# Threshold attention and a quick-GELU feed-forward on one core: the first 512 tokens in one standard block, and a new order of products and scores

## The chip, the core and the metric

The kernel runs on one core of a Trainium2 chip. The metric is device time in microseconds (us) of one execution. The core has five engines with a queue each: TensorE (PE in the profile; its weight loads are PEld), VectorE (DVE), ScalarE (ACT), GpSimd (POOL) and SyncE (SP, which here only starts transfers). Each engine works through its own list of instructions in the order in which the program was built, and waits on semaphores for the others. So an instruction that isn't ready holds up all that stand behind it on its engine.

## The reference

Attention in which only the scores within `tau` of their row's maximum count, and then a feed-forward with the quick GELU. The weights are float64, all else is float32.

```python
def _attn_ref(q, k, v, tau):             # batch 8, heads 8, 576 tokens, head size 64
    scores = q @ k.transpose(0, 1, 3, 2) / np.sqrt(q.shape[-1])
    thresh = np.max(scores, axis=-1, keepdims=True) - tau
    scores = np.where(scores >= thresh, scores, -1000000000.0)
    scores = scores - np.max(scores, axis=-1, keepdims=True)
    attn = np.exp(scores)
    attn = attn / (np.sum(attn, axis=-1, keepdims=True) + 1e-09)
    return attn @ v

x = attn_out.transpose(0, 2, 1, 3).reshape(4608, 512)
h = x @ w_in                             # 512 x 2048
g = h * (1.0 / (1.0 + np.exp(-1.702 * h)))
out = g @ w_out                          # 2048 x 512
```

## The kernel before

The work is cut into 32 head pairs (four to a batch) and 18 feed-forward blocks of 256 tokens. For each pair: scores (line 386 for four key tiles of 128, line 379 for the tail of 64 keys), a copy out of PSUM (`keep`, L405), maxima by column (L419 and some small operations), a subtraction of the threshold (`sub`, L489), a mask and an exponential on ScalarE (L500, L504), the product with the values (L518), and the division, which writes the block's input `xT` (`place_x`, L585). The denominators of the first five pairs come from TensorE (`den`, L518 too), later ones from VectorE.

The float64 weights come in 32 pieces of 128 x 512. Each takes two transfers, four VectorE operations (L325, L339, L343, L351) and one on ScalarE (L333). `w_in` is complete first, then `w_out`.

All engines' work is entered as tasks. A task has an engine, an assumed cost, a rank, the tasks it comes after, and the buffers it takes and gives back. When the program is built, a list scheduler plays the tasks through with the assumed costs. Whenever an engine is free it takes the ready task of the lowest rank, and emits its instructions there and then. The assumed costs therefore decide nothing but the order.

```python
limits = {"psA": 3, "psM": 2, "s_m": 8, ...}        # psA: two PSUM banks each; psM: one bank each
...
FIRST, LAST = -9.0, 1000.0                           # feed-forward products rank last on PE
...
def scores(n, t, c):                                 # one half (288 queries) of a key tile, two heads
    ps = psA.tile([P, 2, 512], FP32, name="ps", tag="ps")
    ...
    for h in range(2):
        nc.tensor.matmul(ps[:, h, 0:SH], lhsT=kT[ts(h, D), ts(t, P)],
                         rhs=qT[ts(h, D), ts(c, SH)], start=True, stop=True)
...
def mm1(blk, j, f):                                  # L600: hidden columns j and j+8 share one bank
    if f == 0:
        hidden[j] = psM.tile([P, BANK], FP32, name="hps", tag="mo")
    for c in range(NDC):                             # 4 products of 256 columns
        nc.tensor.matmul(hidden[j][:, ts(f, BLK)], lhsT=w_in[:, c, ds((f * HF + j) * P, P)],
                         rhs=xTs[blk][:, c, :], start=(c == 0), stop=(c == NDC - 1))

def tanh(j): ...                                     # L609, ACT: th <- hidden bank
def gelu(j): ...                                     # L612, DVE: g <- (th + 1) * hidden; frees the bank

def mm2(i, part):                                    # L622: standard second product, 512 columns
    if part == 0:
        acc[i] = psM.tile([P, d_model], FP32, name="ops", tag="mo")
    for j in range(2 * part, 2 * part + 2):
        nc.tensor.matmul(acc[i], lhsT=g[:, j // HF, j % HF, ts(i, HT)], rhs=w_out[:, j, :], ...)
```

The second product of all blocks but the first is done with seven half-size products in place of eight (Winograd's form of Strassen's scheme). The sums of parts of `w_out` that it needs (`t_sum`, L644, the last of them in place) are made once on GpSimd, the sums of parts of `g` (`s_sums`, `s_last`, L649 to L656) in every block.

```python
def product(x, part):                                # L671: one of seven, in two parts of 4 instructions
    left, right, k, o = PRODUCTS[x]
    if x == k and part == 0:
        banks[k] = psM.tile([P, BANK], FP32, name="ops", tag="mo")
    for j in range(4 * part, 4 * part + 4): ...      # 256 columns each

def feed_forward(blk):
    for j in range(HF):
        for f in range(2):
            ffn.append(task("PE", 1.762, LAST, mm1, blk, j, f, after=..., take=("psM",) if f == 0 else (), ...))
        a = task("ACT", 0.6, FIRST, tanh, j, after=ffn[-1:], take=("io",))
        gelus[j] = task("DVE", 0.69, FIRST, gelu, j, after=[a, ...], give=("psM", "io"))
        ...
    if blk < PLAIN:                                  # PLAIN = 1: block 0 takes mm2 and half, then t_sum
        ...
        return
    order = [(P1, 0), (P2, 0), (P1, 1), (P2, 1)]
    order += [(x, p) for x in (P6, P7, P4, P5, P3) for p in range(2)]
    ...                                              # P1 and P2 each take a psM bank at part 0
```

Of the kernel before, what the change touches and what calls it, by code (L numbers as in the profile page):

```python
# [10 lines left out]
FP32 = mybir.dt.float32  # L11
# [4 lines left out]
ALU = mybir.AluOpType  # L16
# [3 lines left out]
P = 128  # L20
# [10 lines left out]
def kernel(  # L31
# [34 lines left out]
    nc = tc.nc  # L66
    B, H, S, D = q.shape
    d_model, d_ff = moe_w_in.shape
    NPAIR = H // 2
# [5 lines left out]
    BLK = 256  # L75
    BANK = 512
# [52 lines left out]
    for x in ("raw0", "raw1", "qkT0", "qkT1", "mb"):  # L129
# [4 lines left out]

    EARLY = {
        "lower_rows": -1.89,
        "values": 0.42,
        "exps": 0.63,
        "load_qk": -0.91,
        "prep": -1.45,  # L140
        "load_v": 1.46,
        "mask": 0.88,
        "over_groups": -1.9,
        "sub": 0.19,
        "one_group": 0.95,
        "one_row": 0.78,
    }
    LATER = {
        "in_groups": 0.38,
        "mask": -1.46,  # L150
        "scores": 1.23,
        "prep": -1.22,
    }
    CV = {
        "cv_end": -0.76,
        "cv_frac": -1.28,
    }

    def task(engine, cost, rank, f, *a, after=(), take=(), give=(), lag=0.06):
# [72 lines left out]
    def own(n, *pools):  # L232
        return tuple(x + "_apart" for x in pools) if n in APART else pools
# [17 lines left out]
    def load_v(n):  # L251
# [11 lines left out]

    WC = 512
    wide = moe_w_in.dtype != FP32
    NWC = d_ff // WC

    pieces = [
        (w_in, moe_w_in, c, x * NWC // 2 + j)
        for j in range(NWC // 2) for x in range(2) for c in range(NDC)  # L270
    ]
    n_in = len(pieces)
    pieces += [(w_out, moe_w_out, c, j) for c in range(NFC) for j in range(d_model // WC)]
    cv, turn = {}, {"w64": 0}
# [99 lines left out]
    def scores(n, t, c):  # L374
        qT, kT = mats[n, 0], mats[n, 1]
        ps = psA.tile([P, 2, 512], FP32, name="ps", tag="ps")
        if t == NKT:
            for i in range(2):
                nc.tensor.matmul(  # L379
                    ps[:, i, 0:SH], lhsT=kd, rhs=qT[:, ts(i, SH)],  # L380
                    start=True, stop=True,
                )
            del mats[n, 0], mats[n, 1]
        else:
            for h in range(2):
                nc.tensor.matmul(  # L386
                    ps[:, h, 0:SH],
                    lhsT=kT[ts(h, D), ts(t, P)], rhs=qT[ts(h, D), ts(c, SH)],
                    start=True, stop=True,
                )  # L390
        pss[n, t, c] = ps

    def keep(n, t, c):
        if t == NKT:
# [222 lines left out]
    def mm2(i, part):  # L617

        if part == 0:
            acc[i] = psM.tile([P, d_model], FP32, name="ops", tag="mo")  # L620
        for j in range(2 * part, 2 * part + 2):
            nc.tensor.matmul(  # L622
                acc[i], lhsT=g[:, j // HF, j % HF, ts(i, HT)], rhs=w_out[:, j, :],
                start=(j == 0), stop=(j == NFC - 1),
            )

    def half(i):
        osbs[i] = work.tile([P, d_model], FP32, name="osb", tag=f"osb{i}", bufs=1)
        nc.scalar.activation(out=osbs[i], in_=acc.pop(i), func=AF.Copy, scale=0.5)


    qa = [[g[:, f, :, ts(h, HT)] for f in range(2)] for h in range(2)]
    qb = [[w_out[:, ts(f, HF), ts(m, HM)] for m in range(2)] for f in range(2)]
# [29 lines left out]
    ]  # L663
    banks = {}

    def product(x, part):
        left, right, k, o = PRODUCTS[x]
        if x == k and part == 0:
            banks[k] = psM.tile([P, BANK], FP32, name="ops", tag="mo")
        for j in range(4 * part, 4 * part + 4):  # L670
            nc.tensor.matmul(  # L671
                banks[k][:, ts(o, HM)], lhsT=left[:, j, :], rhs=right[:, j, :],
                start=(j == 0), stop=(j == HF - 1),
            )

    def read(x):


        if x == P1:
            for i in range(2):  # L680
                osbs[i] = work.tile([P, d_model], FP32, name="osb", tag=f"osb{i}", bufs=1)
        (c11, c12), (c21, c22) = ([osbs[i][:, ts(m, HM)] for m in range(2)] for i in range(2))
        k, h = PRODUCTS[x][2:]
        ps = banks[k][:, ts(h, HM)]
        if x == P1:
            nc.scalar.activation(out=c21, in_=ps, func=AF.Copy, scale=0.5)
            return
        sums = {
            P6: [(c12, c21)], P2: [(c11, c21)], P7: [(c22, c12)], P4: [(c21, c22)],
            P5: [(c12, c12), (c22, c22)], P3: [(c12, c12)],  # L690
        }
        for o, a in sums[x]:
            nc.vector.scalar_tensor_tensor(  # L693
                out=o, in0=ps, scalar=0.5, in1=a, op0=ALU.mult, op1=ALU.add
            )

    def store(blk, i):
        nc.sync.dma_start(out=out[ds(blk * BLK + i * HT, HT), :], in_=osbs[i])
# [37 lines left out]
    BY_PE = 5  # L736
    BY_DMA = 8
    LEAD = 6

    W_IN, W_OUT = (3.04, 0.51), (2.15, 3.32)  # L740
    ready_w, w_loads = [], []
    for i in range(len(pieces)):
        if i < n_in:
# [20 lines left out]

    placed, ffn = {}, []
    last_mm2, t_ready = {}, []
    PLAIN = 1

    def feed_forward(blk):
        b = -(-(blk + 1) * BLK // S) - 1  # L770
# [2 lines left out]
        for j in range(HF):  # L773
            for f in range(2):
                after = ffn[-1:] + xs[-NPAIR:]
                if blk == 0:
                    x = 2 * (j * P // WC) + f
                    after += ready_w[x * NDC : (x + 1) * NDC]
                last = j == HF - 1 and f == 1
                ffn.append(task(  # L780
                    "PE", 1.762, LAST, mm1, blk, j, f, after=after,
                    take=("psM",) if f == 0 else (), give=("xT",) if last else (),
                ))
            a = task("ACT", 0.6, FIRST, tanh, j, after=ffn[-1:], take=("io",))
            gelus[j] = task(
                "DVE", 0.69, FIRST, gelu, j, after=[a, last_mm2.get(j // 4)],
                give=("psM", "io"),
            )
            if blk >= PLAIN and j % 2:
                sums.append(task("POOL", 2.5, FIRST, s_sums, j // 2, after=[gelus[j - 1], gelus[j]]))  # L790
        if blk < PLAIN:
            for i in range(2):
                for p in range(NFC // 2):
                    after = ffn[-1:] + [gelus[2 * p % HF], gelus[2 * p % HF + 1]]
                    if blk == 0:
                        after += ready_w[n_in + 2 * p : n_in + 2 * p + 2]
                    ffn.append(task(
                        "PE", 1.762, LAST, mm2, i, p, after=after,
                        take=("psM",) if p == 0 else (),
                    ))  # L800
                    last_mm2[p // 2 % 2] = ffn[-1]
                a = task("ACT", 0.6, FIRST, half, i, after=ffn[-1:], take=("osb",), give=("psM",))
                task("SP", 0.6, FIRST, store, blk, i, after=[a], give=("osb",), lag=2.2)
            if blk == PLAIN - 1:

                for x in range(4):
                    for k in range(2):
                        after = t_ready[-1:] + (ffn[-1:] if x == 3 else ffn[16 : 17])
                        t_ready.append(task("POOL", 3.2, FIRST, t_sum, x, k, after=after + ready_w[n_in:]))
            return  # L810
        reads = [None] * 7

        order = [(P1, 0), (P2, 0), (P1, 1), (P2, 1)]
        order += [(x, p) for x in (P6, P7, P4, P5, P3) for p in range(2)]
        for x, p in order:
            after = ffn[-1:] + t_ready
            if x in (P1, P2, P4):
                after += [gelus[j] for j in range(4 * p, 4 * p + 4)]
            elif x == P3:
                after.append(lasts[p])  # L820
            else:
                after += sums[2 * p : 2 * p + 2]

            after += [reads[y] for y in range(x) if PRODUCTS[y][2:] == PRODUCTS[x][2:]]
            ffn.append(task(
                "PE", 1.762, LAST, product, x, p, after=after,
                take=("psM",) if x in (P1, P2) and p == 0 else (),
            ))
            last_mm2[p] = ffn[-1]
            if p == 0:  # L830
                continue
            if x == P6:
                lasts = [task("POOL", 1.6, FIRST, s_last, k, after=ffn[-1:]) for k in range(2)]
# [16 lines left out]
    for n in range(NP):  # L850
# [19 lines left out]
        for t in range(NKT + 1):  # L870
            tail = t == NKT
            copies = []
            for c in range(1 if tail else 2):

                a = task(
                    "PE", (0.97 if tail else 0.53) * slow, r, scores, n, t, c,
                    after=[pq, pk] + ([pd] if tail else []) + after,
                    take=("psA", "s_t") if tail else ("psA",) + (own(n, "s_m") if c == 0 else ()),
                    give=own(n, "qkT0", "qkT1") + ("kd",) if tail else (),
                )  # L880
                after = [a]
                copies.append(task("ACT", 0.65, r, keep, n, t, c, after=[a], give=("psA",)))
            mx.append(task("DVE", 0.76 if tail else 1.37, r, in_groups, n, t, ALU.max, after=copies))
        a = task("DVE", 0.78, r, over_tiles, n, ALU.max, after=mx)
        a = task("DVE", 0.78, r, over_groups, n, ALU.max, after=[a])
# [55 lines left out]
            "DVE", 1.1, r, place_x, n, after=[a, pv], take=("xT",) * len(new), give=("psA", "rc")  # L941
        )
        while hp == NPAIR - 1 and (next_blk + 1) * BLK <= (b + 1) * S:
            feed_forward(next_blk)
            next_blk += 1
    run_in_order()

# [29 lines left out]
```

## Time and profile before

| | |
|---|---|
| time of three runs | 1413.49, 1418.3, 1419.67 us (median 1418.3) |
| profiled execution | 1415.12 us, 1413.3 us from first to last instruction |
| mean granted TensorE clock | 0.982 |
| busy share PE, PEld, DVE, ACT, POOL | 95%, 73%, 75%, 44%, 21% |

How to read it: a group of the profile is a source line on an engine with its tiles, the number of records and their mean time. A float32 matrix product instruction leaves two records, so four instructions show as "x8". "Idle before" names what ended a wait. "PEclk" or "granted clock" is the share of full TensorE speed that the chip allowed in a stretch. Times on the timeline count from the first instruction.

### The profile page before, as it was taken

What the parts mean: (1) busy time and instruction counts of PE and PEld (TensorE: products, weight loads), DVE (VectorE), ACT (ScalarE), POOL (GpSimd) and SP (SyncE); (2) the same over time, 40 slices, a digit from 0 to 9 for tenths busy, and PEclk for the clock granted to TensorE, in tenths of its full rate; (3) what the DMA queues carried; (4) which work ended last, traced back from release to release, by engine and by line L of the source; (5) the groups of instructions that cost most, each with busy time, mean ns of one, the idle gap of its engine ahead of it and who ended that gap; (6) DMA issues with size and microseconds to landing.
All of it is one profiled execution on the core that took longest, in us unless ns stands there. A gap on an engine that the chain in (4) does not pass through costs nothing.

```text
span 1413.3 us, 18181 instructions
## 1 busy us (share of the span) xinstructions
PE 1346.5 (95%) x6904; PEld 1028.8 (73%) x6904; DVE 1063.4 (75%) x1780; ACT 628.9 (44%) x805; POOL 303.8 (21%) x388
## 2 busy tenths in 40 slices
PE   5878897999999999999999999999999999999998
PEld 3436546777777777777777777777777777888887
DVE  7998988889998889887888888788876787111111
ACT  6684554555454545454444355454543453100100
POOL 1222263202021222221221202121201212211211
PEclk9989998999999999999999999999999999999999
DMA  8788743131110111111111110111111000000000
GB/s 184 199 288 259 262 120 69 34 62 30 41 26 27 23 34 32 32 27 26 41 26 41 26 41 16 34 26 37 21 41 26 10 15 8 8 16 8 8 15 15
DMA packets 205727, 79.59 MB, mean 56 GB/s; under 512 B 192840, under 2 KB 192840, under 8 KB 205640
## 3 DMA queue, kind: packets, MB, share of 16 engines
q1 hardware_dynamic: 196072, 44.60, 14.8%
q0 software_dynamic: 7200, 33.55, 7.0%
q8 instruction: 54, 0.88, 0.3%
q10 hardware_dynamic: 2368, 0.30, 0.2%
q14 instruction: 33, 0.27, 0.1%
HBM read 68.93 MB, written 9.47 MB: 55 GB/s over the span
## 4 chain that ended last, share of the span: by engine, by line
PE 76%; DVE 18%; DMA 2%; issue 2%; ACT 1%; SPq 0%; POOL 0%; ACTq 0%; DVEq 0%; POOLq 0%
PE hps L600 28%; PE ops L671 27%; PE pv L518 9%; PE ps L386 9%; DVE s_m L489 4%; PE ps L379 2%; DVE part L419 2%; DVE arena L612 2%; DVE s_t L494 1%; DVE mb L463 1%; DVE red L438 1%; DVE w_out L343 1%; DMA arena<-in_moe_w_out_dram 1%; DVE w_in L351 1%; DVE arena L489 1%
## 5 line engine op out<-in xcount | busy, mean ns | idle before, releaser
L600 PE MATMUL hps<-xT,w_in 128*128 128x256 f32 x2304 | 514.9, 382 | 3.1 <-DVE arena L612 2.8
L600 PEld LDWEIGHTS hps<-xT,w_in 128*128 128x128 f32 x2304 | 434.6, 190 | 79.9 <-issue 14.5
L419 DVE TRANSPOSE_TENSOR_REDUCE part<-s_m 128x36 f32<-128x1152 f32 x228 | 304.3, 1357 | 66.1 <-ACT s_m L405 60.8
L671 PE MATMUL ops<-w_out,arena 128*128 128x256 f32 x1088 | 254.3, 386 | 7.6 <-DVE arena L612 7.3
L405 ACT COPY s_m<-ps 128x576 f32<-128x576 f32 x240 | 140.2, 647 | 231.5 <-PE ps L386 229.9
L671 PEld LDWEIGHTS ops<-w_out,arena 128*128 128x128 f32 x1088 | 206.7, 193 | 48.0 <-DVE arena L612 10.1
L609 ACT ACTIVATE th<-hps 128x512 f32<-128x512 f32 x144 | 85.4, 593 | 309.1 <-PE hps L600 300.8
L500 ACT ACTIVATE s_m<-s_m 128x1152 f32<-128x1152 f32 x120 | 136.7, 1156 | 111.0 <-DVE s_m L489 109.7
L612 DVE SCALAR_TENSOR_TENSOR arena<-th,hps 128x512 f32<-128x512 f32 x144 | 97.3, 675 | 117.2 <-ACT th L609 116.1
L671 PE MATMUL ops<-arena 128*128 128x256 f32 x816 | 184.2, 381 | 0.0
L489 DVE TENSOR_TENSOR s_m<-s_m,mb 128x1152 f32<-128x1152 f32 x120 | 176.5, 1509 | 1.9 <-DMA mb<-row 1.6
L649 POOL TENSOR_TENSOR arena<-arena 128x256 f32<-128x256 f32 x68 | 62.2, 914 | 522.5 <-DVE arena L612 519.9
L386 PE MATMUL ps<-qkT 64*128 64x288 f32 x960 | 150.5, 445 | 23.2 <-DVE qkT L362 14.7
L671 PEld LDWEIGHTS ops<-arena 128*128 128x128 f32 x816 | 154.5, 190 | 24.4 <-issue 3.9
L504 ACT ACTIVATE s_m<-s_m,shift,scl 128x1152 f32<-128x1152 f32 x120 | 157.9, 1339 | 1.1
L386 PEld LDWEIGHTS ps<-qkT 64*128 64x128 f32 x960 | 86.8, 196 | 78.3 <-issue 44.2
L693 DVE SCALAR_TENSOR_TENSOR osb<-ops,osb 128x256 f32<-128x256 f32 x119 | 47.8, 413 | 114.5 <-PE ops L671 110.4
L518 PE MATMUL pv<-s_m,v_m 128*64 128x288 f32 x960 | 126.8, 417 | 0.0
L518 PEld LDWEIGHTS pv<-s_m,v_m 128*64 128x64 f32 x960 | 67.7, 140 | 54.7 <-issue 9.6
L367 POOL COPY kd<-qkT 64x64 f32<-64x64 f32 x60 | 13.9, 232 | 314.3 <-DVE qkT L362 312.5
L656 POOL TENSOR_TENSOR arena<-arena 128x512 f32<-128x512 f32 x34 | 49.6, 1461 | 112.9 <-PE ops L671 112.9
L650 POOL TENSOR_TENSOR arena<-arena 128x256 f32<-128x256 f32 x68 | 60.8, 894 | 5.3
(94 smaller groups left out, 971.1 us busy)
## 6 DMA issues: line engine op xcount, KB each, us to landing
out_dram<-osb SPq DMA_DIRECT2D x36, 256.0 KB, 2.0
q_raw<-in_q_dram SPq DMA_DIRECT2D x120, 72.0 KB, 2.3
k_raw<-in_k_dram SPq DMA_DIRECT2D x116, 72.0 KB, 2.3
v_m<-in_v_dram SPq DMA_DIRECT2D x64, 128.0 KB, 2.4
w_out<-in_moe_w_in_dram POOLq DMA_DIRECT2D x12, 512.0 KB, 9.9
arena<-in_moe_w_out_dram POOLq DMA_DIRECT2D x12, 512.0 KB, 6.1
w_out<-in_moe_w_in_dram POOLq DMA_DIRECT2D x12, 511.6 KB, 10.7
arena<-in_moe_w_out_dram POOLq DMA_DIRECT2D x12, 511.6 KB, 7.2
```

Of the source, the lines that this page charges most:

```text
L386: nc.tensor.matmul(ps[:, h, 0:SH], lhsT=kT[ts(h, D), ts(t, P)], rhs=qT[ts(h, D), ts(c, SH)], start=True, stop=True,)
L405: nc.scalar.copy(out=o, in_=pss.pop((n, t, c))[:, :, 0:SH])
L419: nc.vector.tensor_reduce(out=o, in_=i, axis=AXL.X, op=op, apply_transpose=True)
L489: nc.vector.tensor_tensor(out=s, in0=s, in1=mb, op=ALU.subtract)
L500: nc.scalar.activation(out=s, in_=s, func=AF.Prelu, alpha=STEEP)
L504: nc.scalar.activation(out=s, in_=s, func=AF.Exp, scale=scl, bias=shift)
L518: nc.tensor.matmul(o[c][ts(h, D), 0:SH], lhsT=lhsT, rhs=rhs, start=(t == 0), stop=(t == NKT),)
L600: nc.tensor.matmul(hidden[j][:, ts(f, BLK)], lhsT=w_in[:, c, ds((f * HF + j) * P, P)], rhs=xTs[blk][:, c, :], start=(c == 0), stop=(c == N ...
L609: nc.scalar.activation(out=ths[j], in_=hidden[j], func=AF.Tanh, scale=GELU_SCALE / 2)
L612: nc.vector.scalar_tensor_tensor(out=g[:, :, j, :], in0=two(ths.pop(j)), scalar=1.0, in1=two(hidden.pop(j)), op0=ALU.add, op1=ALU.mult,)
L649: nc.gpsimd.tensor_tensor(out=u1, in0=a21, in1=a22, op=ALU.add)
L671: nc.tensor.matmul(banks[k][:, ts(o, HM)], lhsT=left[:, j, :], rhs=right[:, j, :], start=(j == 0), stop=(j == HF - 1),)
```

## The change

It does three things to the order of the work, and sets new ranks and assumed costs for the scheduler.

1. Blocks 0 and 1 become one block of 512 tokens with standard products. Its hidden columns are made in plain order, both blocks' halves into one bank, and `g0` lies over the space of `t4`, `g` and their sums. So one more block than before does without the seven products. The block opens with 128 TensorE instructions of 256 columns that need `w_in` alone (64 before), ahead of any that need `w_out`. The pieces of `w_in` are loaded in that order of columns. Two of the four `t_sum` pairs must now come after the block's last product, since they write where `g0` lay.
2. In the other blocks the first of the seven products is finished (in parts of 4, 3 and 1 instructions) before the second begins, where the two alternated before.
3. From the seventh pair on (`WHOLE = 6`) both halves of a key tile's scores are one task that takes two `psA` buffers, so that TensorE gets its four instructions in one run.

```diff
     EARLY = {
-        "values": 0.42,  "exps": 0.63,  "load_qk": -0.91,  "prep": -1.45,  "sub": 0.19,  "one_row": 0.78,
+        "values": 1.63,  "exps": 1.38,  "load_qk": -1.15,  "prep": -1.35,  "sub": -0.29,
+        "scores": -0.68,  "spread_sums": 0.92,  "sums_by_pe": 1.09,  "in_groups": 0.61,  "keep": -1.15,
...                                       (entries put on one line here; LATER and CV lose entries)
-    pieces = [
-        (w_in, moe_w_in, c, x * NWC // 2 + j)
-        for j in range(NWC // 2) for x in range(2) for c in range(NDC)
-    ]
+    pieces = [(w_in, moe_w_in, c, j) for j in range(d_ff // WC) for c in range(NDC)]
...
+    g0 = arena[:, ds(2 * HF * HM, 2 * NFC * BLK)].rearrange("p (j t) -> p j t", t=2 * BLK)
+    PLAIN = 2
+
+    def mm1_0(j, i):
+        if i == 0:
+            hidden[j] = psM.tile([P, BANK], FP32, name="hps", tag="mo")
+        for c in range(NDC):
+            nc.tensor.matmul(
+                hidden[j][:, ts(i, BLK)], lhsT=w_in[:, c, ts(j, P)], rhs=xTs[i][:, c, :],
+                start=(c == 0), stop=(c == NDC - 1),
+            )
...
-    W_IN, W_OUT = (3.04, 0.51), (2.15, 3.32)
+    W_IN, W_OUT = (3.21, 1.53), (3.16, 2.2)
...
-                    "PE", 1.762, LAST, mm1, blk, j, f, after=after,
+                    "PE", FFU, LAST, mm1, blk, j, f, after=after,          # FFU = 1.722
...
+        for x in range(4):                                  # in first_blocks()
+            for k in range(2):
+                after = t_ready[-1:] + (ffn[-1:] if x > 1 else ffn[2 * NFC : 2 * NFC + 1])
+                t_ready.append(
+                    task("POOL", 3.0, FIRST, t_sum, x, k, after=after + ready_w[n_in:])
+                )
...
-        order = [(P1, 0), (P2, 0), (P1, 1), (P2, 1)]
-        order += [(x, p) for x in (P6, P7, P4, P5, P3) for p in range(2)]
+        order = [(P1, 0), (P1, 2), (P1, 3)]
+        order += [(x, p) for x in range(P2, 7) for p in range(2)]
         for x, p in order:
+            js = ((0, 4), (4, 8), (4, 7), (7, 8))[p]
...
-            for c in range(1 if tail else 2):
+            if tail or n >= WHOLE:
+                cs = range(1 if tail else 2)
                 a = task(
-                    "PE", (0.97 if tail else 0.53) * slow, r, scores, n, t, c,
+                    "PE", (1.2 if tail else 1.35) * slow, r, scores_of, n, t, cs, ...
-                    take=("psA", "s_t") if tail else ("psA",) + (own(n, "s_m") if c == 0 else ()),
+                    take=("psA", "s_t") if tail else ("psA", "psA") + own(n, "s_m"),
...
+            else:
+                for c in range(2): ...                      # as before, assumed cost 0.6
```

## The prediction

> **What bounds the kernel now.** I read the page's busy line first, then a table by stage, then the timeline of TensorE for the stages in which it was idle.
>
> ```profile
> PE 1346.5 (95%) x6904; PEld 1028.8 (73%) x6904; DVE 1063.4 (75%) x1780; ACT 628.9 (44%) x805; POOL 303.8 (21%) x388
> ...
> PEclk9989998999999999999999999999999999999999
> ```
>
> TensorE is busy 95% of 1413.3 us, so only 67 us of it are idle. What no change of order can remove is the matrix work itself. The stage table (columns: length, then busy us of PE, PEld, DVE, ACT, POOL, then granted clock) shows where the idle time lies:
>
> ```profile
> 60.00:118.00 58.00, 40.65 (x268) 21.86 (x266) 56.42 (x110) 43.52 (x55) 13.59 (x26) 0.89 0.74 235
> 118.00:232.00 114.00, 99.38 (x440) 62.30 (x437) 101.06 (x170) 56.31 (x74) 40.55 (x43) 0.91 0.65 195
> ...
> 400.00:600.00 200.00, 199.89 (x1057) 154.84 (x1056) 175.69 (x295) 100.74 (x126) 46.00 (x49) 1.00 0.15 30
> ```
>
> Before 118 us VectorE is the bound (56.42 of 58 us busy): pairs 0 to 3 and the conversion of the weights must pass it before the first feed-forward product. TensorE's idle time there, 38 us, goes only when VectorE gets shorter. From 232 us on TensorE is nearly full. Between the two lie 14.6 us of idle TensorE (114.00 - 99.38), and the timeline says what ended them:
>
> ```profile
> 123.98 1.99 PE L600 MATMUL hps<-xT,w_in 128*128 128x256 f32 x8
> ...
> 162.07 1.13 PE L622 MATMUL ops<-w_out,arena 128*128 128x512 f32 x2 [1.50 <-DVE w_out L351]
> 167.41 3.78 PE L622 MATMUL ops<-w_out,arena 128*128 128x512 f32 x4 [4.22 <-DVE w_out L351]
> ...
> 222.70 5.84 PE L386 MATMUL ps<-qkT 64*128 64x288 f32 x24 [7.54 <-DVE xT L585]
> ```
>
> The feed-forward begins at 123.98. 5.7 us go to pieces of `w_out` that VectorE has not converted yet, 7.5 to scores that need a `psA` buffer which pair 5's late division still holds. In the rest of the run the idle time is 14.4 us, of which about 3.6 are the last store. Most of what remains is one recurring place, the first two of the seven products:
>
> ```profile
> 1014.24 1.89 PE L671 MATMUL ops<-w_out,arena 128*128 128x256 f32 x8
> 1018.83 6.49 PE L671 MATMUL ops<-w_out,arena 128*128 128x256 f32 x21 [2.70 <-DVE arena L612]
> ```
>
> Eight records, that is the first four instructions of P1, run; then TensorE waits for the last GELU, which alone frees the second bank, for P2.
>
> **What the Trainium skill says.** "SBUF — State Buffer", section "Who interferes with whom": a VectorE instruction with two SBUF inputs contends with a GpSimd instruction that reads SBUF, and the later one blocks wholly. The trace agrees. While GpSimd makes the `w_out` sums (190 to 209 us), the subtraction of pair 5 is stretched:
>
> ```profile
> 192.28 12.14 DVE L489 TENSOR_TENSOR s_m<-s_m,mb 128x1152 f32<-128x1152 f32 x4 [1.61 <-DMA mb<-row]
> ```
>
> against 5.12 us for the same four at 27.82 us. These 7 us delay pair 5, hence the 7.54 us above. "TensorE: Matmul & The Clock Gate", section "What's actually happening": after an idle window of some 3.4 us TensorE runs at half clock until it has been busy about as long. The trace agrees: after 6.2 us of idle time, the 32 score records at 117.23 took 6.82 us (clock 0.64 from 118 to 124), and the same 32 at 16.03 took 4.42.
>
> **The change part by part.** I add up TensorE's work after the first feed-forward product, in the built order of both programs, with times read off undisturbed stretches of the timeline: 0.4316 us per 256-column instruction (27.63 us for 64), 0.864 per 512-column one, 0.25 per value or denominator instruction (5.0 for 20), 0.27 per score instruction plus 0.1 per run of scores (1.17 for four, 3.27 for twelve), 0.2 whenever a full-array product is followed by an attention one (1.93 in place of 1.73 for four).
>
> *Second product of block 1.* 32 x 0.864 = 27.65 us in place of 56 x 0.4316 = 24.17: +3.5.
> *Runs of scores.* The program has 113 runs in place of 92, and 112 changes from feed-forward to attention in place of 105; most but not all lie after the first product: +2.1. Joining the scores from the seventh pair on brings nothing by itself, since the order before has runs of 6, 12 and 16 there as well as of 2.
> *Sum.* 1251.5 us before, 1257.1 after: +5.6, all on the path, as TensorE is the bound there.
> *Start.* By mean times, VectorE has 118.4 us of work up to pair 3's last division where it had 117.1. In addition, its reductions now stand ahead of the wait for pair 1's threshold row (46.9 us), with the 2.1 us of division work behind it. The first block's scores (pair 4), which stood between, now come earlier. I take 123.5 for the first product: -0.5.
> *Idle time from 118 to 232.* The new block has 128 x 0.4316 = 55 us of products that need no `w_out`, plus some 17 us of attention between them, until about 123.5 + 72 = 196 us. VectorE's last piece of `w_out` has 202.3 us of mean-time work ahead of it (186.2 before, which came at 190.5), so it lands near 207. The sixteenth standard product needs it at about 196 + 15 x 0.86 = 209. So the 5.7 us go. The first sums on GpSimd then fall beside reductions in place of subtractions, and most of the 7.5 us go too. But VectorE is full from 120 to 207 us and paces the GELUs within about 1 us of TensorE, so I leave 4 of 14.6 us: -10.6.
> *P1 whole.* P2's bank is now needed after 8 instructions, and the last GELU's data after 7 (3.0 us), where the bank was needed after 4 (1.73 us): 1.3 us more room. The five waits of this kind (0.78, 0.68, 2.70, 2.00, 1.14) shrink to about 0, 0, 1.4, 0.7, 0: -5.
> *Clock.* Before, the sum 124.0 + 1251.5 + 29.0 us of idle time falls 8.8 short of 1413.3. Slow clock is part of it: 0.80 from 220 to 240 us, 0.83 from 160 to 180, behind the waits that now go. I count -3.
>
> Sum: +5.6 - 0.5 - 10.6 - 5 - 3 = -13.5 us, or 1418.3 - 13.5 = 1405 us.
>
> **The rivals.** (a) *VectorE becomes the bound of the first 300 us.* Block 2 needs all of pairs 4 to 7. By VectorE's mean times pair 7 is divided after 271.9 us of work (269.9 before, where it really came at 287.8, 18 us later through waits and the shared port). TensorE reaches block 2 at 123.5 + 156 = 279.5. If the 18 us repeat in full, TensorE waits 10 us there and the result is about 1415. For it: the sums have only moved. Against: 10 of the 18 us were VectorE waiting for TensorE or blocked by GpSimd beside subtractions. (b) *The waits for GELUs stay*, since they come from subtractions that stand in front of a GELU in VectorE's list, and get longer than the room: without the 5 us, 1410. (c) *The late sums hold up block 2's products.* Four `t_sum` now follow the last standard product; at 3.1 us each they take 12.4 us beside the 39 us up to the first of the seven products, so I expect no wait, but subtractions beside them may lose 4 us. (d) *The new ranks make the start worse*: denominators now go first and all masks ahead of the exponentials; each us of delay at 120 us costs one at the end.
>
> **Range and chances.** All idle time and lost clock after 124 us are 38 us. To be faster by over 2% (28 us) the change would have to win back nearly all of it on top of its own 5.6, so 0.07. To be slower by 2% it would need a new wait of 40 us against my sum: 0.03. Rivals (a) and (b) together give about 1420 at worst, and all idle time of both stages removed gives 1394. Range 1392 to 1419.
>
> **What would show it.** Right: first feed-forward product within 2 us of 124; no wait for a `w_out` conversion; under 5 us of TensorE idle time from 118 to 232; after P1, no wait of over 1.5 us for a GELU; tail of four bare blocks unchanged. Wrong: a wait of TensorE for `xT` ahead of block 2 near 280 us (rival a), unchanged total of L612 waits (b), a first product later than 127 (d). A gain far over 13 us would mean that TensorE's work is smaller than I add up.

## The result, and the profile after

The changed kernel takes **1401.62 us** (median of 4 runs, 1401.13 to 1403.66) where the kernel before took 1416.01 us beside it. The ratio is 0.9899 with a 95% interval of 0.987 to 0.9928. So it gains 14.4 us, and 11.4 us between the two profiled spans (1413.3 and 1401.9 us). The lines that answer to those of the prediction: the busy line and the granted clock of the page first.

```profile
PE 1341.3 (96%) x6856; PEld 1012.6 (72%) x6856; DVE 1037.4 (74%) x1773; ACT 625.9 (45%) x806; POOL 281.7 (20%) x374
...
PEclk9869999999999999999999999999999999999999
```

The second dip in the clock row, near 230 us before, is gone, and the one at the start is deeper. The same stages as before (length, then busy us of PE, PEld, DVE, ACT, POOL, then granted clock):

```profile
60.00:118.00 58.00, 32.86 (x196) 17.68 (x194) 40.20 (x79) 33.20 (x43) 7.63 (x16) 0.79 0.64 185
118.00:232.00 114.00, 105.84 (x518) 72.05 (x516) 104.99 (x177) 61.02 (x81) 32.36 (x47) 0.99 0.75 221
...
600.00:1240.00 640.00, 640.00 (x3327) 499.87 (x3326) 501.94 (x849) 291.17 (x373) 128.40 (x156) 1.00 0.13 27
```

Three things are to be seen. From 118 to 232 us TensorE is busy 6.5 us longer and its clock is 0.99 in place of 0.91. From 600 to 1240 us it isn't idle at all. But from 60 to 118 us VectorE, the bound there, is busy for only 40.20 us where it was for 56.42. TensorE's timeline, with its waits in brackets:

```profile
90.27 2.29 PE L382 MATMUL ps<-arena 64*128 64x288 f32 x8 [15.86 <-ACT arena L405]
...
134.88 1.46 PE L640 MATMUL hps<-xT,w_in 128*128 128x256 f32 x6
137.41 19.90 PE L640 MATMUL hps<-xT,w_in 128*128 128x256 f32 x90 [1.07 <-DVE xT L585]
...
227.40 4.30 PE L622 MATMUL ops<-w_out,arena 128*128 128x512 f32 x6 [2.81 <-DVE w_out L347]
...
1012.10 7.07 PE L690 MATMUL ops<-w_out,arena 128*128 128x256 f32 x32
```

The first feed-forward product comes at **134.88**, 10.9 us later than before (123.98). The wait for `w_out` is 2.81 us where there were 5.7, the 7.54 us that scores waited for pair 5's division are gone, and P1 and P2 run through (the last line) where 2.70 us of waiting stood.

Put together in the prediction's own ledger: the span is the start of the first product, then TensorE's busy time, then its idle time. Busy time first (the kernel before, then the changed one, from the first product to the end):

```profile
123.98:1413.30 1289.32, 1260.35 (x6374) 981.12 (x6372) 953.91 (x1582) 542.25 (x696) 278.46 (x324) 0.99 0.17 40
```

```profile
134.88:1401.90 1267.02, 1255.90 (x6321) 965.22 (x6319) 934.31 (x1587) 540.99 (x696) 259.32 (x316) 1.00 0.17 42
```

Part of it is slow clock. After the first product the granted clock is 1 but for these stretches, in which it is 0.50 (third column from the end), so that half of TensorE's busy time there is lost (before, then after):

```profile
166.68:173.51 6.83, 6.09 (x14) 2.37 (x16) 6.83 (x9) 3.94 (x5) 2.59 (x6) 0.50 0.74 183
217.88:228.12 10.24, 5.42 (x23) 4.22 (x24) 9.25 (x30) 2.76 (x5) 0.00 (x0) 0.50 0.06 18
1020.01:1023.43 3.42, 3.42 (x10) 2.71 (x9) 3.23 (x4) 1.01 (x2) 1.07 (x2) 0.50 0.00 0
1098.52:1101.93 3.41, 3.41 (x10) 2.70 (x9) 3.40 (x3) 2.23 (x2) 3.33 (x3) 0.50 0.00 0
```

```profile
228.64:232.05 3.41, 3.41 (x6) 0.97 (x6) 3.41 (x4) 0.52 (x1) 3.41 (x2) 0.50 0.20 77
```

| us | before | after | change | predicted |
|---|---|---|---|---|
| first product | 123.98 | 134.88 | +10.9 | -0.5 |
| work: busy time less the half lost to slow clock | 1251.2 | 1254.2 | +3.0 | +5.6 |
| lost to slow clock | 9.2 | 1.7 | -7.5 | -3 |
| idle, first product to 232 us | 14.6 | 6.4 | -8.2 | -10.6 |
| idle, from 232 us to the last store | 10.7 | 1.1 | -9.6 | -5 |
| last store | 3.7 | 3.7 | 0 | 0 |
| span | 1413.3 | 1401.9 | -11.4 | -13.5 |

It gained although it starts 11 us late.

**Why it starts late.** VectorE's own timeline and SyncE's transfers around the gap, in the changed kernel (SPq: start and length of the issue):

```profile
85.87 5.16 DVE L489 TENSOR_TENSOR s_m<-s_m,mb 128x1152 f32<-128x1152 f32 x4 [15.82 <-DMA mb<-row]
```

```profile
59.22 4.04 SPq L246 DMA_DIRECT2D q_raw<-in_q_dram  x4
63.37 14.82 SPq L246 DMA_DIRECT2D k_raw<-in_k_dram  x4
78.30 0.53 SPq L471 DMA_DIRECT2D row<-flat  x1
82.08 0.36 SPq L480 DMA_DIRECT2D mb<-row  x1
```

VectorE had pair 2's threshold row (`flat`) ready at 62.58 us. It is to go to memory in a row and come back to all partitions (`row`, then `mb`). But on SyncE the eight loads of pair 5's q and k stand ahead of it, and issuing the last four took 14.82 us. The row left at 78.30 and was back at 85.87; until then VectorE, and behind it ScalarE and TensorE, stood still. In the kernel before the row was the later one in SyncE's list too, and yet went out in time, at 65.57 us:

```profile
56.49 5.13 SPq L245 DMA_DIRECT2D k_raw<-in_k_dram  x4
...
65.57 0.46 SPq L471 DMA_DIRECT2D row<-flat  x1
67.24 0.35 SPq L480 DMA_DIRECT2D mb<-row  x1
```

The stage table in steps of 5 us shows the difference in its last columns (DMA busy share and GB/s). Before, from 60 to 70 us:

```profile
60.00:65.00 5.00, 4.96 (x40) 2.68 (x36) 4.68 (x15) 3.29 (x6) 0.00 (x0) 1.00 0.51 91
65.00:70.00 5.00, 4.49 (x28) 2.66 (x28) 4.96 (x12) 4.15 (x8) 2.90 (x6) 1.00 0.52 131
```

and after, from 60 to 70 and 75 to 80 us:

```profile
60.00:65.00 5.00, 3.37 (x26) 1.55 (x22) 4.74 (x15) 0.24 (x1) 1.30 (x3) 1.00 1.01 310
65.00:70.00 5.00, 1.88 (x8) 1.14 (x8) 4.72 (x11) 2.80 (x5) 2.93 (x6) 0.82 1.18 262
...
75.00:80.00 5.00, 0.00 (x0) 0.00 (x0) 0.00 (x0) 0.00 (x0) 0.00 (x0) 0.85 1.05 275
```

Before, the DMA engines had a gap at 60 to 70 us, and the row slipped through it ahead of the weight pieces that GpSimd issued from 67.10 us on. After, they are full from 55 to 80 us, and from 75 to 80 us no engine of the core does anything.

### The profile page after: what moved, and what is told of

It reads as the page before. It is cut to its first block, busy times and chain, and to the rows that moved or that the text cites. A ratio compares the mean times of both kernels' runs of the same rounds, so it can differ in the third digit from the quotient of the medians.

```text
span 1401.9 us, 18089 instructions
## 1 busy us (share of the span) xinstructions
PE 1341.3 (96%) x6856; PEld 1012.6 (72%) x6856; DVE 1037.4 (74%) x1773; ACT 625.9 (45%) x806; POOL 281.7 (20%) x374
## 4 chain that ended last, share of the span: by engine, by line
PE 86%; DVE 7%; DMA 4%; issue 2%; SPq 2%; ACT 0%; POOL 0%; DVEq 0%; POOLq 0%
PE hps L600 32%; PE ops L690 27%; PE pv L518 10%; PE ps L382 9%; PE ops L622 3%; PE ps L375 2%; SPq L246 2%; PE hps L640 1%; DVE s_m L489 1%; DVE part L419 1%; DMA w_out<-in_moe_w_in_dram 1%; DVE arena L489 1%; DMA arena<-row 1%; DMA arena<-in_moe_w_out_dram 1%; DMA w_out<-in_moe_w_out_dram 1%
## 5 line engine op out<-in xcount | busy, mean ns | idle before, releaser
L600 PE MATMUL hps<-xT,w_in 128*128 128x256 f32 x2048 | 457.3, 381 | 0.0
L600 PEld LDWEIGHTS hps<-xT,w_in 128*128 128x128 f32 x2048 | 385.8, 190 | 67.3 <-issue 11.3
L690 PE MATMUL ops<-w_out,arena 128*128 128x256 f32 x1024 | 232.8, 381 | 0.0
L690 PEld LDWEIGHTS ops<-w_out,arena 128*128 128x128 f32 x1024 | 192.8, 190 | 33.6 <-issue 6.2
L668 POOL TENSOR_TENSOR arena<-arena 128x256 f32<-128x256 f32 x64 | 58.5, 915 | 677.0 <-DVE arena L612 677.0
L690 PE MATMUL ops<-arena 128*128 128x256 f32 x768 | 174.3, 381 | 0.0
L489 DVE TENSOR_TENSOR s_m<-s_m,mb 128x1152 f32<-128x1152 f32 x120 | 160.9, 1374 | 16.5 <-DMA mb<-row 15.8
L612 DVE SCALAR_TENSOR_TENSOR arena<-th,hps 128x512 f32<-128x512 f32 x128 | 87.1, 680 | 111.3 <-ACT th L609 109.3
L690 PEld LDWEIGHTS ops<-arena 128*128 128x128 f32 x768 | 144.8, 190 | 24.7 <-issue 4.6
L382 PE MATMUL ps<-qkT 64*128 64x288 f32 x960 | 149.6, 435 | 10.9 <-DVE qkT L358 9.3
L518 PE MATMUL pv<-s_m,v_m 128*64 128x288 f32 x960 | 123.1, 409 | 0.0
L622 PE MATMUL ops<-w_out,arena 128*128 128x512 f32 x128 | 59.4, 613 | 2.8 <-DVE w_out L347 2.8
L670 POOL TENSOR_TENSOR arena<-arena 128x256 f32<-128x256 f32 x64 | 60.3, 941 | 0.0
```

Of the source, the lines that this page charges most:

```text
L489: nc.vector.tensor_tensor(out=s, in0=s, in1=mb, op=ALU.subtract)
L518: nc.tensor.matmul(o[c][ts(h, D), 0:SH], lhsT=lhsT, rhs=rhs, start=(t == 0), stop=(t == NKT),)
L612: nc.vector.scalar_tensor_tensor(out=g[:, :, j, :], in0=two(ths.pop(j)), scalar=1.0, in1=two(hidden.pop(j)), op0=ALU.add, op1=ALU.mult,)
L622: nc.tensor.matmul(acc[i], lhsT=g0[:, j, ts(i, P)], rhs=w_out[:, j, :], start=(j == 0), stop=(j == NFC - 1),)
L690: nc.tensor.matmul(banks[k][:, ts(o, HM)], lhsT=left[:, j, :], rhs=right[:, j, :], start=(j == 0), stop=(j == HF - 1),)
```

## The experiments

Theory A after the result: the change is worth what the prediction says, and more, in the later stages, and loses 11 us at the start to the queued row. Rivals: VectorE's new order or the new ranks make the start late; or the block itself does, through its order of the weight pieces. The parts were also run by themselves. Each ratio below is to the kernel before, run on the same chip; on the three chips used it took 1414.49, 1415.88 and 1420.78 us, so between runs on different chips the ratios and the profiled spans say more than the times.

### The row ahead of the loads (a_row)

```diff
+        rows_first = [row_ins[2]] if n >= 5 else []
-        lq = task("SP", 2.0, r - 2.0, load_qk, n, 0, q0, take=own(n, "raw0"), lag=2.0)
+        lq = task("SP", 2.0, r - 2.0, load_qk, n, 0, q0, after=rows_first, take=own(n, "raw0"), lag=2.0)
         ...                                   # k likewise; row_ins[n] is the task that brings mb
```

> The changed kernel, with the q and k loads of pair 5 and later held until pair 2's threshold row has gone out and come back, so that on SyncE the row stands ahead of pair 5's loads; TensorE's order stays as it is. Theory A (the row waited behind transfers that SyncE could not issue, and this made the first feed-forward product 11 us late): the wait of the subtraction at 85.87 us shrinks from 15.8 us to under 3, the first product comes near 124 in place of 134.9, and the time is near 1391. Rival (the transfer engines are full then, so the row is late wherever it stands): the row still lands after 80 us, time 1400 to 1403.

Measured: **1392.46 us** (1389.73 to 1394.98), ratio 0.9826 (0.98 to 0.9853). The loads give way and the row goes at once:

```profile
63.80 0.30 SPq L471 DMA_DIRECT2D row<-flat  x1
66.10 0.36 SPq L480 DMA_DIRECT2D mb<-row  x1
...
67.80 11.41 SPq L246 DMA_DIRECT2D q_raw<-in_q_dram  x4
```

```profile
74.59 5.16 DVE L489 TENSOR_TENSOR s_m<-s_m,mb 128x1152 f32<-128x1152 f32 x4 [4.40 <-DMA mb<-row]
```

The first product comes at 124.22 and the span is 10.8 us shorter (1391.1), as much as the start had lost. So the late start is this wait: with the row in time, the new order starts where the old one did, as the prediction had assumed. The wait itself, expected under 3 us, is still 4.40: `mb`, issued at 66.10, let VectorE go on only at 74.59. So the rival has a small part in it: among full DMA engines the row is slow even when nothing stands ahead of it in SyncE's list.

### The old ranks (a_ranks)

```diff
-        "values": 1.63, "exps": 1.38, "load_qk": -1.15, "prep": -1.35, "sub": -0.29, "scores": -0.68, ...
+        "values": 0.42, "exps": 0.63, "load_qk": -0.91, "prep": -1.45, "sub": 0.19, ...
-    W_IN, W_OUT = (3.21, 1.53), (3.16, 2.2)
+    W_IN, W_OUT = (3.04, 0.51), (2.15, 3.32)
```

> The changed kernel with the ranks of before (all of its tables and the ranks of the weight loads). SyncE's order of pair 5's loads and pair 2's row is then such that the loads go out some time before the row, as before. Theory A (the new ranks cost the 11 us at the start and bring nothing after it): first product near 124, the time 1392 to 1398, with 4 us more work than the changed kernel's (1261.4). Rival (the new ranks pay for the late start by spacing the work later on): 1401 or more.

Measured: 1404.29 us (1404.85, 1404.07, 1404.51, 1395.16), ratio 0.9867 (0.9834 to 0.9901). The first product came at 136.25, with a wait of 12.93 us for the same row. Here the row left at 69.65, after the loads, and `mb` could be issued only at 82.21. I had blamed the ranks for the late start, and that fell: it is there with the old ones as well.

### The block of 512 tokens alone (b_block), and with the row ahead (b_block_row)

The kernel before with the new first block and order of weight pieces; ranks, single scores, P1 and P2 in turn as before.

```diff
-    PLAIN = 1
+    PLAIN = 2                                 # mm1_0, gelu_0, g0, first_blocks as in the change
+    pieces = [(w_in, moe_w_in, c, j) for j in range(d_ff // WC) for c in range(NDC)]
+    WHOLE = 99
```

> The kernel before with the block of 512 tokens alone: ranks and assumed costs of before, P1 and P2 alternating, separate half tiles of scores. Work after the first feed-forward product adds up to 1256.1 us (1251.5 before). Theory A (the early waits and the slow clock behind them end with it, and the start stays near 124 since SyncE's order is the old one): idle time of TensorE from 118 to 232 us falls from 14.6 to under 6, the clock there rises to 0.98 or more; 8 to 12 us faster than before, near 1406, with waits after P1's first four instructions still there. Rival (the gain was in the ranks): 1414 or more.

Measured: 1406.24 us (1406.46, 1411.43, 1406.03, 1394.95), ratio 0.9881 (0.9834 to 0.9929). The number is the expected one, but not for the reason given: the start was to stay near 124, and the first product comes at 134.14, late again. A larger gain behind it makes up for that. Here pair 5's loads stand where they stood before, but the row goes out at 68.16 us, 2.6 us later than before, behind the pieces of weights issued from 66.46 us on. `mb` then leaves at 75.95 and VectorE waits 11.52 us. So 2.6 us became 10, and the block's order of the pieces is enough to make the row late. One run of four of this kernel, and one of `a_ranks`, is about 10 us shorter than the others. That fits an execution in which the row won that race; it was not traced, so this is argued only.

With pair 5's loads held until the row is out (the edit of a_row):

> The 512-token block alone in the kernel before (ranks, alternating P1 and P2 and single scores as before), but with pair 5's and later loads of q and k on SyncE held until pair 2's threshold row has gone out. TensorE's and VectorE's order as in b_block. Theory A (the late start is pair 2's row falling behind the weight transfers, nothing that VectorE or TensorE has to do): the first feed-forward product comes near 124 in place of 134.1, the wait for the row in the 80s falls from 11.5 us to under 5, and the span falls by 7 to 10 us, to some 1396 us. Rival (the block's order of the weight pieces makes the start late by the conversions themselves): first product stays over 130 and the time over 1402.

Measured: **1397.69 us** (1396.89 to 1398.43), ratio 0.9873 (0.9849 to 0.9897); the profiled span is 8.8 us shorter than without (1395.9 against 1404.7). The two ratios do not show this difference; with one of b_block's four runs 10 us shorter than the rest, its interval is wide. The row's wait is 3.20 us, and the first product comes at 126.85, not quite at the expected 124. The block with the row in time is thus worth some 17 us, more than the whole change showed.

### The first product whole, alone (b_p1) and left out (a_alt)

```diff
-        order = [(P1, 0), (P2, 0), (P1, 1), (P2, 1)]
-        order += [(x, p) for x in (P6, P7, P4, P5, P3) for p in range(2)]
+        order = [(P1, 0), (P1, 1)]            # b_p1, in the kernel before; a_alt undoes it in the one after
+        order += [(x, p) for x in range(P2, 7) for p in range(2)]
```

> The kernel before with nothing changed but that P1 is finished before P2 begins. Its orders on all engines equal the kernel before's through its first 600 us and more. Theory A: the 7.3 us of waits after P1's first four instructions shrink to under 2, and with them some 3.5 us of slow clock; 8 us faster than before, near 1408. Rival: the GELU stands behind subtractions that are longer than the room gained; waits stay at 5 us or more and the time within 2 us of 1416.

Measured: 1408.41 us (1402.88 to 1418.25, 14 runs), ratio 0.9947 (0.9927 to 0.9968). The waits of the first products (group lines of P1 and P2; the last columns are idle time and what ended it) in the kernel before and in b_p1:

```profile
L671 PE MATMUL ops<-w_out,arena 128*128 128x256 f32 x1088 | 254.3, 386 | 7.6 <-DVE arena L612 7.3 <-DVE osb L693 0.3
```

```profile
L671 PE MATMUL ops<-w_out,arena 128*128 128x256 f32 x1088 | 250.1, 382 | 1.6 <-DVE arena L612 1.6
```

The waits fall by 5.7 us, as the prediction's -5 has it. The group's busy time falls as well, by 4.2 us over the same 1088 records. Of these, 3.4 are the two slow stretches at 1020 and 1098 us, which are gone. The profiled execution (1403.28 us) is one of the shorter of the 14, so its span is 11.8 us below that of the kernel before, where the ratio says 7.5.

> The changed kernel, but with P1 and P2 alternating in two parts as before the change. Theory A (P1 whole is what took away the 7 us of waits for the last GELU, and the slow clock after each): waits come back after the first four instructions of P1, 5 to 10 us in total, with clock below 1 after those of over 2 us; 1409 to 1413. Rival (the joined scores or the ranks took them away): within 2 us of 1401.6.

Measured: 1410.45 us (1406.91 to 1412.81), ratio 0.9946 (0.9927 to 0.9965), 8.8 us more than the changed kernel. By the ratios it is 6.7 us. Eleven waits of 0.26 to 0.63 us come back after P1's first four instructions, 5.2 us in sum, none followed by slow clock. The profiled execution (1407.33 us) has a span only 3.6 us longer: -2.4 from an earlier start, +5.1 of late idle time, +3.2 of busy time at full clock, and -2.2 of early idle time and slow clock. Its 15 additional waits explain the +3.2, if each costs 0.26 us besides its length as in s_short below (3.9 by this estimate). What the runs above the profiled one lose stays open.

### Scores not joined (a_split)

```diff
-    WHOLE = 6
+    WHOLE = 99
```

> The changed kernel with the scores of every pair as separate half tiles (as before the change, assumed cost 0.6). TensorE's work after the first feed-forward product adds up to 1251.9 us in place of 1257.1, since scores then come in longer runs. Theory A (joining brings nothing by itself): 1396 to 1402. Rival (joined runs space the scores evenly and so keep GELUs from waiting): waits for GELUs of 5 us or more return, 1403 to 1410.

Measured: 1402.62 us (1400.47 to 1403.63), ratio 0.9897 (0.9869 to 0.9926), the same as the changed kernel within 1 us. TensorE's work added up is 5 us less (1251.9; the trace's 1251.9 against 1254.2, a difference of 2.3, also holds what more waits cost besides their length). But 5.9 us of waits for GELUs are back, 2.5 of them ahead of a first product (L600) and 3.4 within the seven, and two more before scores, 2.3 us in sum, while the early idle time and the slow clock are 5.3 us less. Joining the scores trades one for the other: nothing in the sum.

### What a wait costs, in three sizes (s_short, s_mid, s_long)

Of the slow clock I had counted only a third, so a wait was made on purpose: extra VectorE multiplications by 1 ahead of the last GELU in each of the last four blocks, where TensorE has nothing else.

```diff
     def gelu(j):
+        if j == HF - 1 and late:              # blocks 14 to 17
+            for _ in range(LOOPS):            # 5, 8, 10
+                nc.vector.tensor_single_scalar(out=ths[j], in_=ths[j], scalar=1.0, op=ALU.mult)
```

> The changed kernel with ten multiplications by 1 of the last tanh tile of each of the last four blocks on VectorE, ahead of the last GELU, where VectorE has no other work. It adds no work to TensorE but a wait of about 3 us before the last part of P1, four times over, with nothing else that could change. Theory (a wait of over 2 us costs more than its length, since the clock falls after it): the four waits, 3 us each, cost 12 us plus about 1.7 us each, 17 to 20 us in all; the granted clock is below 1 in the 30 us after each. Rival (the slow clock in the kernel before came of the mix of work and not of the waits): clock 1.00 there and 12 us in all.

Measured with 10: 1424.49 us (1415.83 to 1428.79), ratio 1.0019 (1.0002 to 1.0035); span 22.2 us longer than the changed kernel's. Per wait that is 5.6 us, of which the wait itself is 3.07. Expected were 17 to 20 us: the mechanism was right, its price too low. The twenty runs differ, though, from 1415.83 us at a mean clock of 0.984 to 1428.79 at 0.976; only one of the longer ones was traced.

> The changed kernel with five extra VectorE multiplications by 1 of the last hidden tile before the last GELU in each of the last four blocks (ten gave waits of 3.07 us and 22 us more). If each multiplication is worth 0.33 us, half the number makes the waits about 1.2 us or less. Theory A (waits up to about 1.1 us cost only themselves, longer ones cost their length again in slow clock): span 1402 to 1408, granted clock 0.98 or more in the blocks with a wait. Rival (every wait costs in proportion): clock about 0.94 there, span about 1411.

Measured with 5: 1407.12 us in one run, span 1405.3.

> The same with eight multiplications. Waits of about 2.3 us expected. Theory A: as the waits of 2.0 and 2.7 us in the kernel before, each costs about 2 us again in slow clock: span about 1402 + 4 x 4.3 = 1419, clock 0.92 to 0.95 in the stretches with a wait. Rival (the clock falls only for waits of about 3 us and more): span 1411, clock 0.98 or more.

Measured with 8: 1411.83 us in one run, span 1410.1. The 18 records behind the wait, in s_short, then twice in s_mid, then in s_long:

```profile
1221.72 4.15 PE L698 MATMUL ops<-w_out,arena 128*128 128x256 f32 x18 [0.77 <-DVE arena L620]
```

```profile
1218.96 5.84 PE L698 MATMUL ops<-w_out,arena 128*128 128x256 f32 x18 [2.15 <-DVE arena L620]
1274.87 4.15 PE L698 MATMUL ops<-w_out,arena 128*128 128x256 f32 x18 [2.15 <-DVE arena L620]
```

```profile
1221.74 7.19 PE L698 MATMUL ops<-w_out,arena 128*128 128x256 f32 x18 [3.07 <-DVE arena L620]
```

The time from one block's first product to the next's is 51.80 us in the changed kernel, 52.83 in s_short, 55.90, 54.22 and 55.89 in s_mid, 58.17, 58.10 and 58.06 in s_long. A wait of 0.77 us costs no slow clock, but 0.26 us besides its length. One of 3.07 us makes the same records 3.0 us longer: it costs double, in all four blocks of this execution. One of 2.15 us costs 1.7 us more in the first and third block and nothing in the second and fourth: neither of my two expectations for it.

Why equal waits differ can be read from the clock. "TensorE: Matmul & The Clock Gate", section "What's actually happening", says that activity is judged in windows of some 3.4 us that run freely, and that the clock is halved after at least one idle window. The traces agree on the windows: in all thirteen the granted clock is 1 or 0.50, and changes only at whole multiples of 3.41 us. So the windows' places can be counted off from the changes. The two around the first wait of s_mid (1216.81 to 1218.96 us) and around the second (1272.72 to 1274.87), as in the stage table:

```profile
1216.45:1219.86 3.41, 1.26 (x6) 0.82 (x5) 2.25 (x5) 0.16 (x1) 0.80 (x2) 1.00 0.02 5
1219.86:1223.27 3.41, 3.41 (x10) 2.70 (x9) 0.00 (x0) 0.22 (x1) 1.33 (x2) 0.50 0.00 0
```

```profile
1271.06:1274.47 3.41, 1.66 (x8) 1.12 (x6) 3.10 (x8) 0.00 (x0) 0.00 (x0) 1.00 0.00 0
1274.47:1277.89 3.42, 3.02 (x14) 2.69 (x15) 0.34 (x1) 0.38 (x1) 2.12 (x3) 1.00 0.02 5
```

The first falls whole into one window, and the next runs at half clock: 1.7 us lost. The second is cut by a boundary into 1.75 and 0.40 us, and no slow clock follows. In the thirteen traces, after the first feed-forward product, each window at full clock with 2.00 us of idle time or more is followed by one at half clock, and none with 1.94 us or less is. A window at half clock is followed by another if it has 0.65 us of idle time or more, as the rests of s_long's waits have; those without idle time are followed by full clock. So a whole idle window, as the page has it, is not needed here. And a longer wait can be free: b_block and b_block_row wait 3.13 us at the same place, and only the first, with 2.87 us of it in one window, pays:

```profile
236.77 4.87 PE L381 MATMUL ps<-qkT 64*128 64x288 f32 x24 [3.13 <-DVE xT L584]
```

```profile
229.50 3.33 PE L381 MATMUL ps<-qkT 64*128 64x288 f32 x24 [3.13 <-DVE xT L584]
```

### The sums behind the last conversion (a_hold)

What is left in a_row is a wait of 2.81 us for `w_out`. VectorE's last conversion steps (L335, L339) are stretched there, beside the first sums on GpSimd:

```profile
209.33 2.60 DVE L335 TENSOR_SCALAR arena<-arena 128x512 int32<-128x512 int32 x1
211.96 2.73 DVE L339 SCALAR_TENSOR_TENSOR arena<-arena 128x512 int32<-128x512 int32 x1
```

```profile
209.22 4.93 POOL L663 TENSOR_TENSOR arena<-w_out 128x1024 f32<-128x1024 f32 x2 [7.32 <-DVE w_out L347]
```

So a one-column copy on GpSimd was put ahead of the sums that reads the last piece of `w_out`, and therefore comes after its conversion.

```diff
+    def hold(blk):
+        nc.gpsimd.tensor_copy(out=held, in_=w_out[:, NFC - 1, d_model - 1 : d_model])
 ...
+        t_ready.append(task("POOL", 0.2, FIRST, hold, 0, after=ready_w[n_in:] + ffn[2 * NFC : 2 * NFC + 1]))
```

> a_row with one small GpSimd copy ahead of the sums of parts of w_out, which reads the last column of the last piece of w_out, so that no sum starts before the last conversion is done. Theory A (the first sum blocks the last conversion on VectorE, whose two operations took 2.5 and 2.7 us in place of 0.43 and 0.69, and TensorE waits 2.8 us for that piece): the wait falls under 1 us, the time 2 to 3 us below a_row's, near 1390. Rival (the sums now block subtractions instead, or the last piece is late for another reason): no change within 1 us.

Measured: **1387.34 us** (1386.05 to 1390.42), ratio 0.9767 (0.9744 to 0.9789), the best version, 14.3 us below the changed kernel. The expectation was 2 to 3 us below a_row: it is 5.1 by the times, 3.7 between the spans (1387.4 and 1391.1), though the first product comes 1.9 us later here. The same two steps in it:

```profile
210.45 0.44 DVE L335 TENSOR_SCALAR arena<-arena 128x512 int32<-128x512 int32 x1
210.93 0.69 DVE L339 SCALAR_TENSOR_TENSOR arena<-arena 128x512 int32<-128x512 int32 x1
```

The 4.2 us that they had been stretched are gone, and with them the wait for `w_out` and the slow window behind it.

## Why the prediction was right or wrong

The time came within 3.4 us of the 1405 predicted, by luck: errors nearly cancel. The start was 11.4 us too early and the early idle time 2.4 us too short; against that, the other terms came out 11.7 us better than counted.

- **The start: the step that failed.** "I take 123.5 for the first product: -0.5" stands on VectorE's work in front of it, about as much as before. That was right: up to the end of pair 3's division (at 120.32 and 137.88 us) VectorE is busy 105.85 us before and 106.06 after. What failed is that I counted VectorE's work and not what it waits for. It waited 15.82 us for a row that SyncE could not send, and the start moved by +10.9; a_row, with the row moved and TensorE's order kept, starts at 124.22. My own test, "a first product later than 127 (d)", went off, but rival (d) named the wrong cause: the ranks are not needed for it (a_ranks), and the block alone brings it (b_block). In the profile of before I had seen no wait for that row, and did not ask how near it was to having one.
- **The work: right.** +5.6 by addition, +3.0 in the trace. The addition leaves out what a wait costs besides its length. At 0.26 us each (s_short), the 11 waits fewer after the first product make 2.9 us, by estimate the whole difference.
- **The idle time from 118 to 232: right in kind, short by 2.4.** -8.2 in place of -10.6, so the test of under 5 us of idle time failed. The 7.5 us at `psA` went, as argued, and the sums stood beside reductions without stretching them. But a wait for `w_out` of 2.81 us stayed, against "no wait for a `w_out` conversion". I put the last piece near 207 us. With the late start it was done at 227.34, in a_row at 216.55; 4.2 us of this delay are two conversion steps beside GpSimd's sums, which I had expected to hurt subtractions alone.
- **P1 whole: right in mechanism, term too small.** I left about 2.1 us of the recurring waits; none is there (640.00 of 640.00 us busy). -9.6 in place of -5, of which P1 alone gives 5.7 (b_p1). The rest needs the other parts of the change, and which of them is not settled: a_split shows that joining gives most of it and takes it again as work and as early waits.
- **The clock: right in kind, counted at less than half.** -7.5 in place of -3. I had the 8.8 us that the sum left over in hand (the trace shows 9.2 lost), and the two slow stretches that I named, 0.83 from 160 to 180 and 0.80 from 220 to 240 us, alone cost 3.0 and 2.7 us. The waits of 2.70 and 2.00 us near 1018 and 1097 cost another 1.7 each. What the change leaves is one stretch behind the 2.81 us wait for `w_out`, 1.7 us. I had seen the rule in the 6.2 us gap at 117 us, and did not apply it to the shorter waits that the change takes away.
- **The rivals.** (a) fell: block 2 starts at 299.69 us without a wait, 0.8 us after pair 7's division. Since everything began 11 us later, this says less than it seems, but in a_row, with the start at 124.22, no wait for `xT` stands there either. (b) fell: no wait of L612's GELUs is left; those of the new first block (L646) make waits of 0.39, 1.15 and 0.94 us. (c) did not show: the four late sums hold nothing up. The last four blocks are unchanged, 51.80 us each in both kernels.

How it adds up: +10.9 + 3.0 - 7.5 - 8.2 - 9.6 = -11.4 us between the spans.

## What to carry to other kernels

When an order changes, look not only at the work ahead of the first critical instruction but at the short transfers that others wait for. One that stands behind bulk loads in a queue may be in time by luck, and it is cheap to hold the loads that nobody needs yet. Price a TensorE wait of 2 us or more at up to double its length, and a shorter one at little more than its length: here the price hung on whether some 2 us of it fell into one window of 3.41 us. And when a change comes out as predicted, still compare each term: here a repair of about 10 us and another of about 4 lay hidden behind a right total.

## What the runs showed of the hardware

- Issuing four loads of 72 KB on SyncE took 2.07 us in one place and 14.82 us in another, with the DMA engines full of 512 KB transfers that GpSimd had issued. All that stands behind them in SyncE's list waits as long, also a row of a few KB.
- A wait of TensorE of 2.15 us cost 1.7 us of slow clock in two of four equal blocks and none in the other two; one of 3.07 us cost 3.0 us in all four, one of 3.13 us 1.5 us in b_block and nothing in b_block_row; one of 0.77 us cost none. In thirteen traces half clock followed a full-clock window of 3.41 us when TensorE was idle for 2.00 us or more of it, and not at 1.94 or less. Besides its length, a wait of 0.77 us cost 0.26 us.
- A GpSimd sum stretches VectorE's integer `tensor_scalar` (0.44 to 2.60 us) as it does the two-input operations (0.69 to 2.73). "SBUF — State Buffer", section "Who interferes with whom", says that `tensor_scalar` can run in a mode with two ports and then contends. The trace agrees; I had named the subtractions alone. The reductions beside the sums kept their 1.36 us.
